# The end of the feature stage of a spectral-mixing and GLU kernel: another bank and another order for the left-over rows of the last group

## The chip, the cores and the metric

One core of one Trainium2 chip runs the kernel. The metric is the device time of one launch, in microseconds (us). Five engines work side by side, each in its own program order: TensorE (PE; its weight loads are listed apart as PEld), VectorE (DVE), ScalarE (ACT), GpSimd (POOL) and SyncE (SP), which issues most DMA transfers.

## The reference

A sequence `x` of 2048 tokens with 640 features goes through two residual blocks; all data are 32-bit floats.

```
h   = x + irfft2( rfft2(layernorm(x)) * (w_r + i w_i) )
z   = layernorm(h)
h2  = h + ((z Wg) * (z Wu)) Wd          # Wg, Wu: 640 x 1728, Wd: 1728 x 640
```

The two-dimensional Fourier transforms are done as products with constant tables. Only the first line matters here, and of it the filter (the product with `w_r + i w_i`), the inverse transform over the sequence and the beginning of the inverse transform over the features.

## The kernel before, in words

The spectral block has these stages. First, for 16 token tiles `t`, a product over the 128 tokens of a tile (line 261, `s1_mm`). Then the stage that the change touches: a loop over 16 groups `g` of frequencies (lines 569 to 646). For one group it does

- `d_mm(g)`: the transform over the features, into two PSUM banks with the tags `re` and `im`;
- `d_out(g)`: ScalarE copies them to SBUF;
- `s2_mm(g)`: the transform over the sequence within the group (line 465), two results of 128 x 322 for the two halves `h` of a group. For the last two groups, 14 and 15, they lie in banks `re` (half 0) and `im` (half 1);
- the filter: `y = v * w` (the direct product), the crossed product `us`, and their sum `y + us` (the join). For groups 0 to 13 this is `filt`. For the last two it is `filt_half` (line 493), by halves: half 1 of group 14 and half 0 of group 15 have the crossed product made by two ScalarE copies (lines 507, 508) and one GpSimd product (line 509), with the direct product on VectorE (line 498); half 0 of group 14 and half 1 of group 15 are done wholly on VectorE (lines 501 to 505);
- `is2_mm(g)`: the inverse transform within the group (line 512). For each half, one product for the 65 left-over rows, into `pr`, and two for the 128-row main parts, into `pm`. Group 14 takes `y` and `us` as two summands, so it needs no join and has 12 products; group 15 has 6. Each 32-bit product stands as two weight loads and two matmuls in the trace;
- `is2_parts(g)`: the results go from PSUM to SBUF. `main` (m) copies `pm` to `qm` on ScalarE; `high` (h) writes the rounded left-over rows to `qr`; `low` (l) writes the rest, `pr - high`, on VectorE; `end` (e) copies the 65th row on ScalarE; `edges` (g) splits that row in two. In the code the five of group 14 are `h0, e0, l0, m0, g0`, those of group 15 `h1, e1, l1, m1, g1`.

The next stage is the inverse transform over the features, for token tiles `t` (lines 721 to 763). `id_mm(0)` is its first work on TensorE: four products that read the columns of all groups in `qm` (8 loads and matmuls), then five that read `qr`, the last three of them with the 65th row. Its result has the tag `eo`, a pair of banks.

PSUM has eight banks. `banks(key, name)` (line 93) closes the pool that had the key and opens another in its place; key `a` is the left half, key `y` the right. In the feature stage pool `a` holds two banks of tag `re` and two of `im`, pool `y` one bank of `im2`, one of `ir2` and the pair `u`. Before the change `is2_mm(15)` writes `im2` and `ir2`, as did `is2_mm(13)`; `is2_mm(14)` writes the pair `u`. Pool `a` is closed and opened anew for `eo` at line 876, after all the lines of the change; pool `y` at line 877. The pools are opened with `tc.tile_pool(name=..., bufs=2, space=..., side=...)` and nothing more.

The order is written by hand: each engine runs its instructions in the order of the code. In the last turn of the loop (`g` = 14) it is: `s2_mm(14)`, `s2_mm(15)`, the filter of 14's half 0 with `is2_out(12)` inside it, `is2_mm(13)`, the three other halves of the filter, `is2_out(13)`; then `is2_mm(14)`, `is2_mm(15)` and the lines 636 to 645.

Of the kernel before, what the change touches and what calls it, by code (L numbers as in the profile page):

```python
# [19 lines left out]
NG = 16  # L20
# [58 lines left out]
def tile_spectral_glu(ctx: ExitStack, tc: tile.TileContext, x, wre, wim, wgu, wlast, wdown, wdlast,  # L79
                      cc, ci, fmain, frem, imain, irem, mm, out):  # L80
    nc = tc.nc
# [18 lines left out]
    def bank(tag, bufs=2):  # L100
        return pools["y" if tag in ("im2", "ir2") else "a"].tile([P, 512], F32, tag=tag, name=tag, bufs=bufs)
# [10 lines left out]
    def wk(shape, name):  # L112
        return work.tile(shape, F32, tag="wk", name=name)
# [20 lines left out]
    def home(tag, shape, name, dt=F32):  # L134
        return keep.tile(shape, dt, tag=tag, name=name)

    def cut(t, o, *shape):
        v = t[:, o:o + int(np.prod(shape))]
        names = [f"d{i}" for i in range(len(shape))]
        return v.rearrange(f"p ({' '.join(names)}) -> p {' '.join(names)}", **dict(zip(names[1:], shape[1:])))  # L140
# [156 lines left out]
    def rest_high(a, b):  # L297
        act(s1r[:, 0, a:b], rest[:, a:b], AF.Copy)

    def rest_low(a, b):  # L300
        tt(s1r[:, 1, a:b], rest[:, a:b], f32(s1r[:, 0, a:b]), op=OP.subtract)
# [15 lines left out]
    for ts, when, aside, root in GROUPS:  # L317
        k = len(when)
        fs, cs = front(ts, k)
        late = []  # L320
# [84 lines left out]
    def load_w(g):  # L405
        w, j = wts[:, g % 3], g // 2 if g < NG - 2 else g - 7
        i = wts[:, 5 if j == 8 else 3 + j % 2]
        nc.sync.dma_start(w, wre[g])
        if g % 2 == 0 or g >= NG - 2:
            nc.sync.dma_start(i, wim[j])  # L410
        W2[g] = w, i

    def load_mm(g, way):
        if g < NG:
            nc.sync.dma_start(mms[g % 4][:, way], mm[g][:, way])
# [10 lines left out]
    def d_mm(g):  # L426
        ps = PD[g] = bank("re"), bank("im")
        where = ((1, 0), (0, 0), (1, 160), (0, 160))
        main = [(b, o, FW[c], s1[:, c, g], fmt[:, FOFF[c]:FOFF[c] + FW[c]]) for c, (b, o) in enumerate(where)]
        if g not in ST:  # L430
            parts(ps, main, [(b, s1r[:, k, g], frt[:, l, b]) for k, l in ((0, 0), (0, 1), (1, 0)) for b in range(2)])
            return
        parts(ps, main, [])
        for q, ((b, o), w) in enumerate(zip(RWHERE, RW)):
            a = 4 * NQ + sum(RW[:q])
            mmx(ps[b][:, o:o + w], ST[g][0:99, q], frall[0:99, a:a + w], False, q >= 2)
# [28 lines left out]
    def s2_mm(g):  # L465
        if g >= NG - 2:
            ps = PU[g] = bank("re"), bank("im")
        elif g == 0:
            ps = PU[g] = bank("im2", 1), bank("ir2", 1)
        else:  # L470
            PU[g] = pools["y"].tile([P, 2, 512], F32, tag="u", name="u", bufs=1)
            ps = PU[g][:, 0], PU[g][:, 1]
        for h in range(2):
            nc.tensor.matmul(ps[h][:, 0:NQ], mms[g % 4][:, 0, h], T[g][:, h], start=True, stop=True)  # L474

    def filt(g):
        w, i = W2[g][0], W2[g][1][64 * (1 - g % 2):64 * (2 - g % 2)]
        y = Y[g] = wk([P, 2, NQ], "y")
        us = wk([P, 2, NQ], "us")

        def products(h, v):
            tt(y[:, h], v, w[:, h], op=OP.mult)
            nc.vector.scalar_tensor_tensor(us[0:64, h], v[64:128], -1.0, i[:, h], op0=OP.mult, op1=OP.mult)
            tt(us[64:128, h], v[0:64], i[:, h], op=OP.mult)

        if g:
            products(slice(0, 2), PU[g][:, :, 0:NQ])
        else:
            for h in range(2):
                products(h, PU[g][h][:, 0:NQ])  # L490
        return lambda: (tt if g else nc.gpsimd.tensor_tensor)(y, y, us, op=OP.add)

    def filt_half(g, h, alone=False, mid=()):
        if h == 0:
            Y[g] = wk([P, 2, NQ], "y"), wk([P, 2, NQ], "us")
        y, us = (a[:, h] for a in Y[g])
        v, w, im = PU[g][h][:, 0:NQ], *W2[g]
        direct = lambda: tt(y, v, w[:, h], op=OP.mult)
        join = lambda: tt(y, y, us, op=OP.add)
        if alone:  # L500
            direct()
            for f in mid:
                f()
            nc.vector.scalar_tensor_tensor(us[0:64], v[64:128], -1.0, im[64:128, h], op0=OP.mult, op1=OP.mult)
            tt(us[64:128], v[0:64], im[0:64, h], op=OP.mult)
            return direct, join
        act(us[0:64], v[64:128], AF.Copy, scale=-1.0)
        act(us[64:128], v[0:64], AF.Copy)
        nc.gpsimd.tensor_tensor(us, us, im[:, h], op=OP.mult)
        return direct, join  # L510

    def is2_mm(g):
        if g == NG - 2:
            both = pools["y"].tile([P, 2, 512], F32, tag="u", name="u", bufs=1)
            pm, pr = both[:, 0], both[:, 1]
        else:
            pm, pr = bank("im2", 1), bank("ir2", 1)
        PI[g] = pm, pr

        def o(ps, n, c, h):  # L520
            return ps[0:n, c * 256:(c + 1) * 256].rearrange("p (a m) -> p a m", m=8)[:, :, 4 * h:4 * h + 4]

        def mm(out, h, a, b):
            ys = [Y[g]] if g < NG - 2 else Y[g] if g == NG - 2 else Y[g][:1]
            for n, y in enumerate(ys):
                nc.tensor.matmul(out, y[:, h, a:b], inv(g, h), start=n == 0, stop=n == len(ys) - 1)  # L526

        if g < NG - 2:
            for h in range(2):
                mm(o(pr, 65, 0, h), h, 128, 193)  # L530
        for h in range(2):
            if g >= NG - 2:
                mm(o(pr, 65, 0, h), h, 128, 193)
            mm(o(pm, P, 0, h), h, 0, 128)
            mm(o(pm, P, 1, h), h, 193, 321)

    def inv(g, h):
        return mms[g % 4][:, 1, h].rearrange("p (a m) -> p a m", m=4)
# [22 lines left out]
    def is2_out(g):  # L561
        high, end, low, main, edges = is2_parts(g)
        high(copy)
        end(copy)
        low()
        main(slice(0, 4))
        edges(nc.gpsimd)
# [11 lines left out]
    for g in range(NG - 1):  # L579
        s2_mm(g)  # L580
        load_mm(g + 4, 0)
        if g + 2 < NG:
            d_mm(g + 2)
        if g + 3 == NG:
            xt = home("big", [P, 2, 5, 2, 512], "xt", F32R)
            flat = xt[:, 1].rearrange("p k l n -> p (k l n)")
            irt, sirt = cut(flat, 0, 5, NQ), cut(flat, 5 * NQ, 4, 162)
            scrap, near = cut(flat, 2258, D), cut(flat, 2258 + D, 4, 4, P)
        if g == NG - 2:
            nc.gpsimd.dma_start(flat[:, 0:2258], irem)  # L590
        if g == NG - 2:
            s2_mm(g + 1)
            filt_half(g, 0, True, (lambda: is2_out(g - 2),))
        if g >= 1:
            is2_mm(g - 1)
            load_mm(g + 3, 1)
        if g < NG - 2:
            add = filt(g)
        else:
            late = [filt_half(g, 1), filt_half(g + 1, 0), filt_half(g + 1, 1, True)]  # L600
            for f in (late[0][0], late[1][0], late[1][1], late[2][1]):
                f()
        if g + 3 < NG:
            load_w(g + 3)
        if g >= 4 and g in AGAIN:
            stack(*AGAIN[g])
        if g == 0:
            rest_high(MID, NG)
        elif g == 1:
            rest_low(MID, NG)  # L610
            qr = home("qr", [P, 2, NT, P], "qr", F32R)
        if g + 2 < NG:
            d_out(g + 2, (0,))
            if 1 <= g < NG - 3:
                high, end, low, main, edges = is2_parts(g - 1)
                high(copy)
                end(copy)
            d_out(g + 2, (1,))
            add()
            if 1 <= g < NG - 3:  # L620
                low()
                main(slice(0, 4))
                edges(nc.gpsimd)
        elif g == NG - 2:
            is2_out(g - 1)
        if g < 2:
            stack(*AGAIN[g])
        elif g == 2:
            spread(MID, NG)
        if g == 9:  # L630
            nc.sync.dma_start(cit, ci)
            nc.sync.dma_start(imt, imain)
# [3 lines left out]
    h0(copy)  # L636
    e0(copy)
    m0(slice(0, 4))
    h1(nc.vector.tensor_copy)
    l0()  # L640
    g0(nc.gpsimd)
    l1()
    m1(slice(0, 2), slice(2, 4))
    e1(copy)
    g1(nc.vector)
    make_identity(nc, ident)
# [289 lines left out]
    late = None  # L936
    for t in range(NT):
# [27 lines left out]
        if t == NT - 2:  # L965
            late = gate_parts(NC - 1, 0)
# [227 lines left out]
    for n, (blk, p) in enumerate(steps):  # L1194
        if p == 6:
            if blk == 0:
# [15 lines left out]
                late = gate_parts(NC - 2, 0)  # L1212
# [4 lines left out]
                late = gate_parts(NC - 1, 1)  # L1217
# [6 lines left out]
            else:  # L1224
# [60 lines left out]
                late = gate_parts(NC - 1, 0)  # L1285
# [15 lines left out]
                late = gate_parts(NC - 2, 0)  # L1301
# [250 lines left out]
```

## Time and profile before

| what | value |
|---|---|
| median of 3 runs | 673.8 us (673.65 to 674.02) |
| the profiled execution's own time | 673.84 us |
| its span, first to last instruction | 672.1 us |
| TensorE busy | 662.1 us (99%) |
| VectorE / ScalarE / GpSimd busy | 470.4 / 322.9 / 393.1 us |
| granted TensorE clock, mean | 1.000 |

Times in the trace count from the span's start. A row of the timeline gives the start and the length in us, the engine, the line, the operation with what it writes and reads, how many instructions are merged, and in brackets how long the engine stood idle just before and what ended that. Most matmuls stand under the line of a helper (L119).

### The profile page before, as it was taken

How to read it: one execution, taken by the hardware profiler on the slowest of the kernel's cores; microseconds unless marked ns; L12 is line 12 of the kernel's file. 1: busy time of each engine (PE TensorE's matmuls, PEld its weight loads, DVE VectorE, ACT ScalarE, POOL GpSimd, SP SyncE). 2: the span in 40 equal slices, each digit the busy share in tenths (PEclk: the TensorE clock that was granted, in tenths of full speed). 3: DMA queues.
4: the chain of work that ended last, by engine and by line, in shares of the span. 5: the costliest groups of instructions: out<-in, count | busy, mean ns of one | idle time of the engine just before them, and what ended most of it. 6: DMA issues, size and time to landing. Idle time of an engine off the chain costs nothing.

```text
span 672.1 us, 10248 instructions
## 1 busy us (share of the span) xinstructions
PE 662.1 (99%) x3695; PEld 587.1 (87%) x3695; DVE 470.4 (70%) x952; ACT 322.9 (48%) x622; POOL 393.1 (58%) x377
## 2 busy tenths in 40 slices
PE   6999999999999999999999999999999999999997
PEld 6999989888888888888888899788888888888887
DVE  6969996788757868594858566754747575756654
ACT  6977773585525253463626146634434252525220
POOL 3101224750397978878787445198787878787610
PEclk9999999999999999999999999999999999999999
DMA  9639885502212121042332467212002121212004
GB/s 320 224 113 283 246 249 149 157 1 79 78 40 79 39 79 35 16 115 53 102 74 79 99 134 257 79 40 78 11 29 79 40 78 40 79 40 80 1 1 156
DMA packets 48953, 66.12 MB, mean 98 GB/s; under 512 B 24082, under 2 KB 30670, under 8 KB 48774
## 3 DMA queue, kind: packets, MB, share of 16 engines
q1 hardware_dynamic: 48246, 62.91, 30.3%
q0 software_dynamic: 288, 2.16, 0.8%
q8 instruction: 29, 0.48, 0.3%
q10 hardware_dynamic: 368, 0.39, 0.2%
q14 instruction: 22, 0.18, 0.1%
HBM read 54.61 MB, written 10.84 MB: 97 GB/s over the span
## 4 chain that ended last, share of the span: by engine, by line
PE 95%; ACT 2%; DVE 2%; DMA 1%; issue 0%; DVEq 0%
PE e L119 50%; PE d L119 26%; PE eo L119 4%; PE y L119 2%; PE re L119 2%; PE u L474 2%; PE im L119 2%; PE im L526 2%; PE im L268 2%; PE ir L526 1%; DMA x<-in_x_dram 1%; ACT s L294 1%; ACT fold L210 0%; ACT fold L209 0%; PE y L792 0%; ACT bits L283 0%
## 5 line engine op out<-in xcount | busy, mean ns | idle before, releaser
L119 PE MATMUL e<-xt,wst 128*128 128x512 f32 x864 | 213.2, 391 | 0.0
L119 PEld LDWEIGHTS e<-xt,wst 128*128 128x128 f32 x864 | 159.8, 188 | 30.6
L1071 DVE TENSOR_TENSOR x<-d,x 128x320 f32<-128x320 f32 x280 | 123.4, 483 | 51.6 <-PE d L119 47.4
L119 PE MATMUL d<-wd,ht 128*128 128x320 f32 x832 | 143.6, 308 | 0.0
L119 PEld LDWEIGHTS d<-wd,ht 128*128 128x128 f32 x832 | 131.1, 188 | 7.6
L985 POOL TENSOR_TENSOR wst<-raw,wst 128x1024 fp32r<-128x1024 f32 x23 | 55.4, 2410 | 67.6 <-ACT wst L984 49.6
L119 PE MATMUL e<-t,wst 128*128 128x512 f32 x360 | 94.3, 392 | 0.0
L119 PEld LDWEIGHTS e<-t,wst 128*128 128x128 f32 x360 | 66.3, 188 | 12.6
L119 PE MATMUL d<-wt,ht 128*128 128x320 f32 x360 | 69.5, 310 | 0.0
L1001 POOL TENSOR_TENSOR wst<-raw,wst 128x896 fp32r<-128x896 f32 (+1 forms) x46 | 65.1, 1439 | 0.2 <-ACT wst L996 0.2
L119 PEld LDWEIGHTS d<-wt,ht 128*128 128x128 f32 x360 | 57.3, 188 | 2.4
L1087 ACT ACTIVATE ht<-e 128x512 fp32r<-128x512 f32 x44 | 26.4, 599 | 51.4 <-DVE e L1150 25.9
L1126 ACT ACTIVATE h<-e 128x512 f32<-128x512 f32 x24 | 14.3, 595 | 66.8 <-PE e L119 66.8
L1046 DVE TENSOR_TENSOR x<-d,x 128x320 f32<-128x320 f32 x62 | 27.5, 485 | 23.1 <-PE d L119 23.1
L996 ACT ACTIVATE wst<-raw 128x896 fp32r<-128x896 f32 (+1 forms) x48 | 30.2, 677 | 27.2 <-POOL raw L990 26.5
L677 ACT ACTIVATE wd<-draw 128x320 fp32r<-128x320 f32 (+1 forms) x30 | 15.7, 558 | 57.1 <-POOL draw L687 54.3
L119 PE MATMUL e<-xt,wdir 128*128 128x512 f32 x180 | 42.4, 393 | 0.0
L119 PEld LDWEIGHTS e<-xt,wdir 128*128 128x128 f32 x180 | 33.3, 188 | 8.1 <-ACT xt L802 0.5
L1146 DVE TENSOR_TENSOR e<-e,h 128x512 f32<-128x512 f32 x24 | 16.8, 699 | 30.8 <-PE e L119 17.8
L1090 DVE TENSOR_TENSOR ht<-e,ht 128x512 fp32r<-128x512 f32 x54 | 36.9, 685 | 1.6 <-ACT ht L1087 1.3
L656 POOL TENSOR_TENSOR wd<-draw,wd 128x640 fp32r<-128x640 f32 x8 | 12.4, 1579 | 40.9 <-ACT wd L655 40.9
L1143 ACT ACTIVATE h<-e 128x512 f32<-128x512 f32 x24 | 14.3, 597 | 40.1 <-PE e L119 40.1
(236 smaller groups left out, 1187.6 us busy)
## 6 DMA issues: line engine op xcount, KB each, us to landing
raw<-in_wgu_dram SPq DMA_DIRECT2D x24, 640.0 KB
draw<-in_wdown_dram SPq DMA_DIRECT2D x24, 320.0 KB
wts<-in_wre_dram SPq DMA_DIRECT2D x16, 322.0 KB
x<-in_x_dram SPq DMA_DIRECT2D x15, 320.5 KB
out_dram<-x SPq DMA_DIRECT2D x15, 320.0 KB
bits<-in_mm_dram SPq DMA_DIRECT2D x32, 128.0 KB
wts<-in_wim_dram SPq DMA_DIRECT2D x9, 322.0 KB
zfar<-zr SPq DMA_DIRECT2D x32, 80.0 KB
```

Source lines behind the costliest of these rows:

```text
L119: nc.tensor.matmul(o, l, r, start=start, stop=stop, skip_group_check=True)
L526: nc.tensor.matmul(out, y[:, h, a:b], inv(g, h), start=n == 0, stop=n == len(ys) - 1)
L677: act(o[:, 0, a:a + n], src, AF.Copy)
L985: ptt(wa[:, 1], stage[:, 0:1024], f32(wa[:, 0]), op=OP.subtract)
L996: act(ws[:, 0, o:o + b - a], stage[:, a:b], AF.Copy)
L1001: ptt(ws[:, 1, o:o + b - a], stage[:, a:b], f32(ws[:, 0, o:o + b - a]), op=OP.subtract)
L1046: tt(xv, ps[b][:, 0:320], xv, op=OP.add)
L1071: tt(xv, o, xv, op=OP.add)
L1087: act(hop[:, a, 0], src, AF.Copy)
L1090: engine.tensor_tensor(hop[:, a, 1], src, f32(hop[:, a, 0]), op=OP.subtract)
L1126: act(h0, oa, AF.Copy)
L1146: tt(ob, ob, h1, op=OP.add)
```

## The change

`is2_mm(15)` takes a bank of tag `im` for `pr` instead of `ir2`, and in its second half the products for the left-over rows come last. In the filter, the direct product of group 14's half 1 is put on VectorE ahead of the work for group 15. At the end, `h1` goes behind `l0` and `m1`.

```diff
@@ is2_mm
         else:
-            pm, pr = bank("im2", 1), bank("ir2", 1)
+            pm, pr = bank("im2", 1), bank("ir2", 1) if g < NG - 1 else bank("im")
@@
         for h in range(2):
-            if g >= NG - 2:
+            last = g == NG - 1 and h
+            if g >= NG - 2 and not last:
                 mm(o(pr, 65, 0, h), h, 128, 193)
             mm(o(pm, P, 0, h), h, 0, 128)
             mm(o(pm, P, 1, h), h, 193, 321)
+            if last:
+                mm(o(pr, 65, 0, h), h, 128, 193)
@@ the loop over g
         else:
-            late = [filt_half(g, 1), filt_half(g + 1, 0), filt_half(g + 1, 1, True)]
-            for f in (late[0][0], late[1][0], late[1][1], late[2][1]):
+            direct, _ = filt_half(g, 1)
+            direct()
+            late = [filt_half(g + 1, 0), filt_half(g + 1, 1, True)]
+            for f in (*late[0], late[1][1]):
                 f()
@@ after the loop
     m0(slice(0, 4))
-    h1(nc.vector.tensor_copy)
     l0()
     g0(nc.gpsimd)
+    m1(slice(0, 2), slice(2, 4))
+    h1(nc.vector.tensor_copy)
     l1()
-    m1(slice(0, 2), slice(2, 4))
     e1(copy)
     g1(nc.vector)
```

## Rows read from the trace of the kernel before

**Rows 1.** The page's part 1: busy time of each engine.

```profile
PE 662.1 (99%) x3695; PEld 587.1 (87%) x3695; DVE 470.4 (70%) x952; ACT 322.9 (48%) x622; POOL 393.1 (58%) x377
```

**Rows 2.** Busy time in stretches: length, PE, PEld, DVE, ACT, POOL, clock, DMA share, GB/s.

```profile
107.10:152.00 44.90, 44.90 (x281) 39.82 (x282) 35.58 (x83) 25.90 (x55) 26.12 (x32) 1.00 0.35 98
```

**Rows 3.** Timeline of TensorE's weight loads at the end of the feature stage.

```profile
102.48 0.30 PEld L526 LDWEIGHTS u<-bits,y 128*128 128x128 f32 x2
102.70 0.30 PEld L526 LDWEIGHTS u<-bits,us 128*128 128x128 f32 x2
103.20 0.19 PEld L526 LDWEIGHTS u<-bits,y 128*65 128x65 f32 x2 [0.19 <-DVE y L498]
...
105.05 0.19 PEld L526 LDWEIGHTS ir<-bits,y 128*65 128x65 f32 x2 [0.50 <-DVE qr L559]
...
107.07 0.98 PEld L119 LDWEIGHTS eo<-tab,qm 128*128 128x128 f32 x7 [0.66 <-ACT qm L552]
```

**Rows 4.** The chain that ended last, same stretch: start, length, what.

```profile
106.15 0.46 PE im L526 x4
...
106.63 0.39 ACT qm L552
...
107.07 7.62 PE eo L119 x52
```

**Rows 5.** Timeline of VectorE, same stretch.

```profile
101.12 0.49 DVE L498 TENSOR_TENSOR y<-im,wts 128x322 f32<-128x322 f32 x1
...
102.65 0.49 DVE L498 TENSOR_TENSOR y<-im,wts 128x322 f32<-128x322 f32 x1
103.06 0.48 DVE L498 TENSOR_TENSOR y<-re,wts 128x322 f32<-128x322 f32 x1
103.65 0.90 DVE L499 TENSOR_TENSOR y<-y,us 128x322 f32<-128x322 f32 x2
104.58 0.42 DVE L559 TENSOR_TENSOR qr<-ir,qr 64x256 fp32r<-64x256 f32 x1
106.19 0.42 DVE L558 CAST qr<-ir 64x256 fp32r<-64x256 f32 x1 [1.19 <-PE ir L526]
...
106.98 0.41 DVE L559 TENSOR_TENSOR qr<-ir,qr 64x256 fp32r<-64x256 f32 x1
107.80 0.21 DVE L555 CAST qr<-bits 1x128 fp32r<-1x128 f32 x1 [0.42 <-ACT bits L541]
108.05 0.28 DVE L556 TENSOR_TENSOR qr<-bits,qr 1x128 fp32r<-1x128 f32 x1
```

**Rows 6.** Timeline of ScalarE, same stretch.

```profile
100.70 0.43 ACT L508 ACTIVATE us<-im 64x322 f32<-64x322 f32 x1
...
104.78 0.38 ACT L541 ACTIVATE qr<-u 64x256 fp32r<-64x256 f32 x1 [1.43 <-PE u L526]
...
105.46 0.60 ACT L552 ACTIVATE qm<-u 128x512 f32<-128x512 f32 x1
...
107.50 0.27 ACT L541 ACTIVATE bits<-ir 1x128 f32<-1x128 f32 x1 [0.21 <-POOL qr L555]
```

**Rows 7.** Timeline of GpSimd: the crossed products of 14's half 1 and 15's half 0.

```profile
101.26 1.72 POOL L509 TENSOR_TENSOR us<-us,wts 128x322 f32<-128x322 f32 x2 [0.32 <-POOL qr L556]
```

**Rows 8.** Timelines at the next closing of pool `a`, where `gu` opens the third stage.

```profile
150.33 0.70 ACT L802 ACTIVATE xt<-y 128x640 fp32r<-128x640 f32 x1 [0.85 <-PE y L792]
...
150.40 0.81 DVE L763 TENSOR_TENSOR x<-eo,x 128x640 f32<-128x640 f32 x1
...
151.33 3.29 PEld L119 LDWEIGHTS e<-xt,wdir 128*128 128x128 f32 x15 [0.46 <-ACT xt L802]
```

**Rows 9.** Who waited for whom on SP's queue, 95 to 135 us: total, times, longest.

```profile
SPq L705 <- DVE qr L558: 9.2, 1, 9.2
```

**Rows 10.** An idle stretch early in the span: stretch by stretch (columns as rows 2), TensorE's timeline.

```profile
10.00:12.00 2.00, 0.46 (x4) 0.49 (x5) 1.90 (x11) 1.97 (x7) 0.74 (x2) 1.00 1.04 395
...
11.54 1.60 PE L268 MATMUL im<-bits,fold 128*128 128x128 f32 x12 [1.55 <-DVE bits L285]
```

## The prediction, made before the changed kernel ran

> **What bounds the kernel now.** I read the busy times first: TensorE works 99% of the span [rows 1]. Then the stretches: from 107.10 to 152.00 it is busy for 44.90 of 44.90 us [rows 2]. So once `id_mm(0)` has begun, at 107.07, nothing but TensorE sets the pace, and what moves that start moves the end by as much. The question is therefore only when `id_mm(0)` starts. The weight loads just before it show three waits [rows 3]: the second half of `is2_mm(14)` (103.20) for a direct product of VectorE, `is2_mm(15)` (105.05) for the `low` of group 13, and `id_mm(0)` (107.07) for ScalarE's `m1`. The reader is to see that each wait is short (0.19, 0.50 and 0.66 us in these rows). The change aims at the first two; the third then has another cause.
>
> **The change part by part.** It removes and adds no instruction and no transfer; it moves some. I follow each engine.
>
> *The direct product of 14's half 1.* It stood at 102.65 and goes to the place at 101.12 [rows 5]. It reads a bank that ScalarE copies from until 100.70 + 0.43 = 101.13 [rows 6], so it starts at about 101.16, against VectorE's turn at 101.12: 0.04 us lost. Queued behind it are the three VectorE steps of 15's half 1, then 15's direct product and the joins. From the first of the five filter steps to the first join it was 103.65 - 101.12 = 2.53 us [rows 5]; the same five instructions stand there in another order, so the join comes at 103.69. Pairs of steps follow each other by 0.41 (102.65 to 103.06) up to 0.59 (103.06 to 103.65), so I allow 0.1 more: 103.69 to 103.80. It ends 0.49 later, at 104.18 to 104.29.
>
> *The second half of `is2_mm(14)`.* Its direct product is now there at 101.65, its crossed product at 102.12, half of GpSimd's 1.72 us from 101.26 [rows 7]. Two loads start every 0.22 us (102.48, 102.70), so the next was due at 102.92 and came at 103.20 [rows 3]: 0.28 us are won. `is2_mm(14)` ends that much earlier: ScalarE, which followed it at 104.78 [rows 6], can go at 104.50, and TensorE's next load is due 12 x 0.11 after 102.92, about 104.2.
>
> *`is2_mm(15)` in another bank.* It no longer waits for the `low` of group 13 (104.58 + 0.42 = 105.00 [rows 5]); the reader of the `im` bank that it takes is the product moved ahead, done by 101.65. What is late next is the first join: 104.18 to 104.29, and 0.06 to the load (102.65 + 0.49 = 103.14 to 103.20 above). So it starts at 104.24 to 104.35 and not at 105.05, 0.70 to 0.81 us earlier. The second join, 0.41 behind the first, is there before the sixth load. The end, 106.61 [rows 4], becomes 105.80 to 105.91, now with `pr` last; `pm` is ready two loads, 0.22 us, earlier. The order inside costs nothing by itself.
>
> *`m1`.* ScalarE needs from 104.78 to 105.46 + 0.60 = 106.06 for group 14 [rows 6]; 0.28 us earlier, it is free at 105.78, when `pm` is ready (105.58 to 105.69). So `m1` starts at 105.79 instead of 106.63. From there to `id_mm(0)` it was 0.44 us [rows 4]: by the data of `qm`, `id_mm(0)` could start at 106.23, 0.84 us earlier.
>
> *The pool.* Here I choose. `pr` of group 15 lay in pool `y`, which is not needed again before `is1_mm(0)`. Now it lies in pool `a`, and pool `a` is closed and opened anew directly ahead of `id_mm(0)`. The pools are opened without the argument `reuse_waits`, whose default is "pool" (the other value is "tile"): what takes the place of a closed pool waits for the readers of all its tiles. The trace has one such switch where the readers come late [rows 8]: the first load of `gu` came at 151.33, its data from ScalarE were there at 151.03, and VectorE's last read of the closed pool's `eo` ended at 150.40 + 0.81 = 151.21, 0.12 us ahead. The row names ScalarE, which had been done for 0.30 us; the reader of the closed pool is the closer one. So the last reader of `pr` gates `id_mm(0)`. That reader is `e1`, behind `l1`, behind `h1`:
>
> - `h1` follows the end of `pr` by 0.03, as `m1` followed 106.61 [rows 4]: 105.83 to 105.94, and takes 0.42 [rows 5];
> - `l1` needs its output. Between a VectorE step and the next that reads it there are 0.04 us (107.80 + 0.21 to 108.05) to 0.11 (103.06 + 0.48 to 103.65) [rows 5]: 106.29 to 106.47, and takes 0.41. Before, `l0` filled this gap, and `l1` came 0.79 behind `h1`; now 0.46 to 0.53;
> - `e1` came 0.11 behind the end of `l1` (106.98 + 0.41 = 107.39 to 107.50 [rows 5, 6]), though the row names GpSimd: 106.81 to 106.99, and takes 0.27;
> - TensorE follows by 0.05 (105.00 to 105.05 [rows 3, 5]) to 0.12 [rows 8]: **107.13 to 107.38**, against 107.07.
>
> So of 0.84 us nothing is left, and 0.06 to 0.31 us are lost. I take 0.15, near the low end, since the same pair `l1`, `e1` stands in the rows and the small gaps are those of single waits.
>
> *What else is moved.* `l0` goes ahead of `h1`, to about 105.1, and with it GpSimd's `g0`, which waits for it: earlier by over 1 us, and nobody waits. `g1` (0.21 + 0.28 on VectorE [rows 5]) ends near 107.6; its readers on TensorE come after the eight loads on `qm`, over 0.9 us behind 107.13, so it stays covered. If `id_mm(0)` began at 106.23 that cover would shrink to nothing and cost some 0.1 us. SP's queue is moved past nothing: its spread of `qr` waited 9.2 us for `h1` [rows 9] and starts 0.3 us earlier, with TensorE never idle in that stretch [rows 2]. Nothing is gained there.
>
> *The sum.* The profiled execution took 673.84 us, 0.04 above the median of 673.8. +0.15 on it is 673.99, or **673.95** as a median.
>
> **The rivals.** *Bank by bank.* The wait at the switch is only for the banks that `eo` takes: `id_mm(0)` begins at 106.23, and 0.84 less 0.1 for `g1` leaves -0.75, 673.05. For it speaks that in rows 8 the late reader may have sat in the very bank that the first load needed, so those rows can't tell bank from pool. Against it speaks the default named above. The Trainium skill's page "PSUM — Partial Sum Buffer", section on bank collisions, asks to guard PSUM by bank and quadrant, which is this rival's rule; no row here shows which one the program keeps.
>
> *Slower: the clock.* TensorE would stand still from 105.85 to 107.2, some 1.35 us in one piece, where before it had waits of 0.50 and 0.66 us with work between them [rows 3]. If the granted clock fell from 2.4 to 1.2 GHz, the products behind it, 7.62 us from 107.07 to 114.69 [rows 4], could take up to twice as long, so up to 681.4; a fifth of that would be enough to be seen. It decides from an idle stretch longer than the trace already has: early in the span TensorE idled 1.55 us, and the clock of that stretch is 1.00 [rows 10], the upper level. The Trainium skill's page "TensorE: Matmul & The Clock Gate", Part 1, says that throttled is the default state and that activity releases it, which speaks against any change that gathers idle time. By rows 10 the gap is too short.
>
> *The change does not do what it says.* The join may come so late that `is2_mm(15)` gains nothing; then the chain to `e1` would end about 0.7 us later, at 107.9 to 108.1, and the time would be about 674.7. The five steps of VectorE [rows 5] speak against it.
>
> **How the numbers follow.** The pool's wait, with +0.06 to +0.31, has 0.83; bank by bank 0.11; the late join 0.03; the clock 0.02; 0.01 is left for a gain beyond all this. A measurement of this kernel can tell about 0.2% from no change, 1.35 us. The pool's wait, the bank rival (-0.75) and the late join (+0.9) lie within that. So within 0.2% has 0.97, slower 0.02, faster 0.01. The likeliest case has 673.7 to 674.3, with the spread of the runs before (673.65 to 674.02) around 673.95. The range takes in the bank rival and ends short of the late join: 672.9 to 674.5.
>
> **What would show it.** Right: the first direct product near 101.16, the joins from about 103.7, `is2_mm(15)` at 104.2 to 104.4 with no wait for a `low`, `m1` at 105.8, and then the first load on `eo` at 107.1 to 107.4, some 0.1 us behind `e1`. Wrong: that load at 106.2 to 106.4 while `l1` or `e1` still runs (bank by bank), matmuls longer than before with a clock under 1.00, or `is2_mm(15)` at 105 again.

## The result and the profile after

The changed kernel took 674.7 us (median of 22 runs, 674.27 to 675.22), the kernel before, beside it on the same chip, 673.65 (22 runs). The ratio is 1.0014, with a 95% interval of 1.0008 to 1.002. By the 0.2% of the prediction that is no difference; but the interval lies wholly above 1, so a small loss is there. The time lies 0.2 us above the predicted range. The profiled execution took 675.22 us, with a span of 673.4.

The busy times first, then two stretches. Page, part 1, and the windows of the kernel after (columns as in [rows 2]):

```profile
PE 662.0 (98%) x3695; PEld 587.2 (87%) x3695; DVE 470.3 (70%) x952; ACT 322.7 (48%) x622; POOL 393.0 (58%) x377
...
107.90:152.80 44.90, 44.90 (x281) 39.81 (x282) 35.27 (x82) 25.32 (x53) 24.99 (x29) 1.00 0.34 98
105.90:107.90 2.00, 0.23 (x3) 0.00 (x0) 1.27 (x4) 1.04 (x4) 1.34 (x5) 1.00 0.02 7
```

Every engine works as long as before, within 0.2 us [rows 1], and behind `id_mm(0)` TensorE is busy for 44.90 of 44.90 us as it was [rows 2]. New is the second window: TensorE has work for 0.23 of 2.00 us. The clock in it, and behind it, is 1.00.

**A measure that does not depend on the launch.** The starts of two profiled executions differ by some tenths of a microsecond for reasons that lie ahead of the change. So everything here counts from the first product of `s2_mm(14)`, which stands ahead of all that is changed. TensorE's timeline, the kernel before, then its weight loads at `id_mm(1)`:

```profile
98.20 0.71 PE L474 MATMUL re<-t,bits 128*128 128x322 f32 x2
...
108.87 1.16 PEld L119 LDWEIGHTS eo<-tab,qm 128*128 128x128 f32 x8
```

The same for the kernel after, with the loads of `is2_mm(14)`, `is2_mm(15)`, `id_mm(0)` and `id_mm(1)`, then the first products of `id_mm(0)`:

```profile
98.47 0.71 PE L474 MATMUL re<-t,bits 128*128 128x322 f32 x2
...
103.20 0.25 PEld L526 LDWEIGHTS u<-bits,y 128*65 128x65 f32 x2
...
104.53 1.36 PEld L526 LDWEIGHTS im<-bits,y 128*65 128x65 f32 x12
107.90 1.12 PEld L119 LDWEIGHTS eo<-tab,qm 128*128 128x128 f32 x8 [2.02 <-ACT bits L544]
108.97 0.77 PEld L119 LDWEIGHTS eo<-xt,qr 128*128 128x128 f32 x5
109.70 0.47 PEld L119 LDWEIGHTS eo<-tab,qm 128*128 128x128 f32 x3
...
107.90 1.37 PE L119 MATMUL eo<-tab,qm 128*128 128x161 f32 x8 [1.77 <-ACT bits L544]
```

I call two distances the *stretch*: to the first load of `id_mm(0)`, before 107.07 - 98.20 = 8.87 [rows 3], after 107.90 - 98.47 = 9.43; and to the first load of `id_mm(1)`, 10.67 and 11.23. Both grew by 0.56 us. The two waits of [rows 3] at 103.20 and 105.05 are gone; at `id_mm(0)` stands one of 2.02 where it was 0.66 (1.77 for the products, which end later than their loads), and what ended it is ScalarE's `end` of group 15 (L544, the `e1` of the prediction).

Who made `e1` late is in the chain of waits of the kernel after (start, length, what):

```profile
105.52 0.60 ACT qm L555
...
106.15 0.42 DVE qr L562
...
106.60 0.43 DVE qr L561
...
107.05 0.43 DVE qr L562
...
107.58 0.28 ACT bits L544
...
107.90 0.68 PE eo L119 x3
```

It reads: ScalarE's `m0`, then VectorE's `l0`, `h1`, `l1`, then `e1`, then `id_mm(0)`. VectorE's timeline shows the same link from its side:

```profile
101.44 0.89 DVE L498 TENSOR_TENSOR y<-im,wts 128x322 f32<-128x322 f32 x2
...
103.97 0.90 DVE L499 TENSOR_TENSOR y<-y,us 128x322 f32<-128x322 f32 x2
104.90 0.42 DVE L562 TENSOR_TENSOR qr<-ir,qr 64x256 fp32r<-64x256 f32 x1
106.15 0.42 DVE L562 TENSOR_TENSOR qr<-u,qr 64x256 fp32r<-64x256 f32 x1 [0.83 <-ACT qm L555]
106.60 0.42 DVE L561 CAST qr<-im 64x256 fp32r<-64x256 f32 x1
107.05 0.42 DVE L562 TENSOR_TENSOR qr<-im,qr 64x256 fp32r<-64x256 f32 x1
```

VectorE is free at 105.32, and `l0` (reads `u`) waits 0.83 us for ScalarE's `m0`. `m0` reads `u` too: its `pm` and the `pr` that `l0` needs are the two banks of one tile of group 14. In the kernel before the same `l0` came behind `h1`, with no wait of its own:

```profile
106.64 0.42 DVE L559 TENSOR_TENSOR qr<-u,qr 64x256 fp32r<-64x256 f32 x1
```

ScalarE's timeline of the kernel after gives `m0`, `m1` and `e1`:

```profile
105.52 0.60 ACT L555 ACTIVATE qm<-u 128x512 f32<-128x512 f32 x1
106.01 0.66 ACT L555 ACTIVATE qm<-im 128x256 f32<-128x256 f32 x2
107.58 0.27 ACT L544 ACTIVATE bits<-im 1x128 f32<-1x128 f32 x1 [0.92 <-DVE qr L562]
```

**A second loss, 180 us later.** 0.56 us is not all: the medians are 1.05 us apart here, and 0.82 in a repeat. Following one and the same instruction through both traces, the distance stays at 0.80 to 0.83 from 108 us on, and jumps to 1.14 near 286 us. VectorE's timeline in the third stage (the products with `Wg`, `Wu` and `Wd`), with the product of TensorE that comes behind it, the kernel before, then after:

```profile
284.53 0.69 DVE L1156 TENSOR_TENSOR h<-e,h 128x512 f32<-128x512 f32 x1 [0.61 <-PE e L119]
285.33 0.70 DVE L1158 TENSOR_TENSOR e<-e,h 128x512 f32<-128x512 f32 x1
...
291.57 0.68 PE L119 MATMUL d<-wt,ht 128*128 128x320 f32 x3
```

```profile
285.33 0.69 DVE L1161 TENSOR_TENSOR h<-e,h 128x512 f32<-128x512 f32 x1 [0.62 <-PE e L119]
286.47 0.70 DVE L1163 TENSOR_TENSOR e<-e,h 128x512 f32<-128x512 f32 x1 [0.46 <-DVE h L1161]
...
292.72 0.68 PE L119 MATMUL d<-wt,ht 128*128 128x320 f32 x3 [0.21 <-DVE x L1076]
```

The second of the two followed the first by 0.80 us and now follows by 1.14, though it waits for nothing but VectorE itself. VectorE is then behind with `x`, and TensorE waits for `x` at 292.72, where before it did not. The change edits nothing in this stage. It does alter the number of VectorE's instructions ahead of this place: the compiled program has 1153 of them instead of 1151. The two more are instructions that only wait on a semaphore, which neither count nor show in the rows. In the trace of the kernel after, one of them stands just ahead of the moved direct product, the other just ahead of `l0`.

### The profile page after: what moved, and what is told of

It is laid out like the page before. It is cut to its first block, busy times and chain, and to the rows that moved or that the text cites. A ratio compares the mean times of both kernels' runs of the same rounds, so it can differ in the third digit from the quotient of the medians.

```text
span 673.4 us, 10250 instructions
## 1 busy us (share of the span) xinstructions
PE 662.0 (98%) x3695; PEld 587.2 (87%) x3695; DVE 470.3 (70%) x952; ACT 322.7 (48%) x622; POOL 393.0 (58%) x377
## 4 chain that ended last, share of the span: by engine, by line
PE 89%; ACT 3%; DVE 3%; DMA 3%; POOL 1%; issue 1%; SPq 0%; DVEq 0%; ACTq 0%
PE e L119 47%; PE d L119 24%; PE eo L119 4%; PE y L119 2%; PE re L119 2%; PE u L474 2%; PE im L119 2%; PE im L526 2%; PE im L268 2%; DMA z<-zfar 1%; PE ir L526 1%; DMA raw<-in_wgu_dram 1%; DMA x<-in_x_dram 1%; ACT s L294 1%; ACT fold L210 0%
```

## The experiments

Twelve kernels ran, each with 11 timed runs beside 33 of the kernel before. This table sums them up; the sections after it give edit, expectation and reading. "Stretch" is to `id_mm(0)` and to `id_mm(1)`; "sum" is the second stretch less 10.67, plus 0.33 where VectorE's gap near 286 us is there (the distance above grows by that, from about 0.81 to 1.14); "time" is the median less that of the kernel before (673.70 in the first four, 673.74 in the next four, 673.73 in the last).

| run | stretch | VectorE instr. | gap | sum | time | ratio, 95% |
|---|---|---|---|---|---|---|
| a1 after again | 9.43, 11.23 | 1153 | yes | +0.89 | +0.82 | 1.0002 to 1.002 |
| a2 `h1` first | 9.00, 10.80 | 1152 | no | +0.13 | +0.12 | 0.9993 to 1.0011 |
| a3 waits by tile | 7.97, 10.51 | 1153 | yes | +0.17 | +0.17 | 0.9992 to 1.001 |
| a4 both | 7.97, 10.43 | 1152 | no | -0.24 | -0.16 | 0.9989 to 1.0006 |
| b1 bank alone | 9.10, 10.90 | 1151 | no | +0.23 | +0.28 | 0.9993 to 1.0011 |
| b2 bank back | 8.69, 10.81 | 1153 | yes | +0.47 | +0.50 | 0.9999 to 1.0016 |
| b3 before, plus 2 | 8.86, 10.66 | 1153 | yes | +0.32 | +0.42 | 0.9997 to 1.0014 |
| b4 after, plus 1 | 9.42, 11.23 | 1154 | no | +0.56 | +0.51 | 1.0 to 1.0017 |
| c1 direct alone | 8.91, 10.70 | 1152 | no | +0.03 | -0.07 | 0.999 to 1.0008 |
| c2 `pr` last | 7.97, 10.37 | 1152 | no | -0.30 | -0.39 | 0.9984 to 1.0002 |
| c3 `pr` last, `l1` first | 7.97, 10.44 | 1152 | no | -0.23 | -0.31 | 0.9985 to 1.0003 |
| c4 `l0` ahead of `m0` | 9.01, 10.80 | 1153 | yes | +0.46 | +0.40 | 0.9996 to 1.0014 |

Most single intervals take in 1, so one time alone says little. That the sum out of the traces and the median agree within 0.10 us in all twelve is what carries the reading.

### The change again, and `h1` ahead of `l0`

The changed kernel once more 

> The changed kernel once more, as a yardstick for the three beside it. In its first profile the stretch from the first product of s2_mm(14) to the first load of id_mm(0) was 9.43 us (98.47 to 107.90) against 8.87 before (98.20 to 107.07), and to the first load of id_mm(1) 11.23 against 10.67: +0.56 us in the stretch. The median was 1.05 us above before. Theory 1 (all of the loss is in the stretch): 0.5 to 0.6 us over before, and the 0.5 us more that the first profile shows behind 107.9 (at about 290 us and at the turn of the blocks at about 400 us) were chance. Theory 2 (part of it comes later, each time): again about 1 us, with steps of 0.2 to 0.4 us behind id_mm(0).

And with `l0` behind the work on group 15:

```diff
     m0(slice(0, 4))
-    l0()
-    g0(nc.gpsimd)
     m1(slice(0, 2), slice(2, 4))
     h1(nc.vector.tensor_copy)
     l1()
+    l0()
+    g0(nc.gpsimd)
     e1(copy)
```

> The changed kernel with h1 and l1 ahead of l0 on VectorE. Theory (l0 waits for ScalarE's m0, and h1 and l1 stand behind it, so e1, for which the new pool waits, comes late): h1 starts right behind the end of is2_mm(15), about 7.70 us into the stretch instead of 8.13, l1 at 8.16, e1 at 8.7, the first load of id_mm(0) at 9.0 instead of 9.43; the time is 0.4 to 0.45 us below the changed kernel, still 0.1 to 0.6 above before. Rival (id_mm(0) is held by something other than the chain h1, l1, e1): the first load stays at 9.4 and the time with the changed kernel's.

The repeat has the same stretches, 9.43 and 11.23, and the same gap, so the second theory holds: part of the loss comes later, each time. With `h1` first the stretch is 9.00, 0.43 shorter. The weight loads of that run:

```profile
107.50 1.12 PEld L119 LDWEIGHTS eo<-tab,qm 128*128 128x128 f32 x8 [1.58 <-ACT bits L544]
```

`e1` still ends the wait. So 0.43 of the 0.56 us is `l0`'s place, and 0.13 remains for the way over `h1`, `l1`, `e1` that the prediction had priced at 0.15. That the time fell by more than 0.43 (from +0.82 to +0.12) is the gap near 286 us: it is gone in this run, which has one VectorE instruction less, the wait ahead of `l0`.

### The pool's wait taken away

All PSUM pools are opened with the argument that lets the wait at a closing go tile by tile:

```diff
-            tc.tile_pool(name=name, bufs=2, space=bass.MemoryType.PSUM, side="right" if key == "y" else "left"))
+            tc.tile_pool(name=name, bufs=2, space=bass.MemoryType.PSUM, side="right" if key == "y" else "left",
+                         reuse_waits="tile"))
```

> The changed kernel with the PSUM pools opened with reuse_waits="tile", so that a new pool's tile waits for the readers of what lay in its own banks only. Theory (the pool as a whole is waited for): id_mm(0) starts behind m1, 8.0 us into the stretch instead of 9.43, but its last three products then wait for g1, so that id_mm(1) starts at 10.6 instead of 11.23: 0.6 us below the changed kernel, about level with before. Rival (the wait was for the bank, not the pool): nothing changes, 9.43 and 11.23 stay.

Weight loads of this run:

```profile
106.33 1.12 PEld L120 LDWEIGHTS eo<-tab,qm 128*128 128x128 f32 x8 [0.56 <-ACT qm L556]
107.41 0.32 PEld L120 LDWEIGHTS eo<-xt,qr 128*128 128x128 f32 x2
108.46 0.45 PEld L120 LDWEIGHTS eo<-xt,qr 128*128 128x128 f32 x3 [0.74 <-POOL ident masks.py:199]
108.87 1.16 PEld L120 LDWEIGHTS eo<-tab,qm 128*128 128x128 f32 x8
```

`id_mm(0)` now follows `m1`, and the stretch falls from 9.43 to 7.97: the wait of 2.02 us was the closing of pool `a`. But the third load of `qr`, one that needs the 65th row, stands still for 0.74 us. The row names GpSimd; the step that makes what the load reads is VectorE's `g1`, which ends about 0.1 us ahead of it in this trace. So of 0.90 us gained at `id_mm(0)` (7.97 against 8.87 before) only 0.16 is left at `id_mm(1)`, and VectorE's gap (0.33) takes more than that.

Both edits together:

> Both: h1 and l1 ahead of l0, and waits tile by tile. Theory: id_mm(0) starts at 8.0, g1 ends about 9.6 us into the stretch, so the last three products of id_mm(0) wait little, and id_mm(1) starts at 10.1 to 10.2 against 10.67 before and 11.23 after: 1.0 to 1.1 us below the changed kernel and about 0.5 below before. Rival (the two edits remove the same wait and don't add up): level with the better of the two alone.

The stretch is again 7.97; `id_mm(1)` is at 10.43, later than expected, and the time is 0.16 us under before instead of 0.5. `g1` began 0.44 us earlier than with the waits by tile alone, but ended only 0.08 earlier: its two steps took 0.34 and 0.56 us (see the last section).

### The bank alone, and all but the bank

The kernel before with only the bank changed:

```diff
-            pm, pr = bank("im2", 1), bank("ir2", 1)
+            pm, pr = bank("im2", 1), bank("ir2", 1) if g < NG - 1 else bank("im")
```

> The kernel before, with one edit: `pr` of group 15 lies in the bank `im` (pool `a`) instead of `ir2` (pool `y`). Measured from the first product of `s2_mm(14)` to the first load of `id_mm(0)`: 8.87 us in the kernel before, 9.43 in the one after. Theory (the switch of pool `a` waits for the last reader of `pr` of group 15, `e1`, behind `l1`): `is2_mm(15)` no longer waits for the `low` of group 13 and starts about 104.5 instead of 105.05, but `h1`, `l0`, `l1` and `e1` must now be over before `id_mm(0)`: h1 105.9, l0 106.4, l1 106.8, e1 107.3 to 107.6, `id_mm(0)` about 107.65. The stretch becomes 9.4 to 9.6, the time 0.5 to 0.7 us more than before. VectorE has as many instructions as before (1151), so its extra gap near 286 us should be absent. Rival (the new order of work on VectorE and TensorE costs the time, not the bank): the stretch is 8.87 or shorter and the time that of before or less.

The kernel after with only that line undone:

> The kernel after, with `pr` of group 15 back in the bank `ir2` (pool `y`). Theory: nothing of pool `a` is read late any more, so the first load of `id_mm(0)` waits for `m1` (ScalarE) and not for `e1`; in exchange `is2_mm(15)` waits again for the `low` of group 13 (about 105.3 on the clock of the kernel after, 0.85 us later than there). Stretch to `id_mm(0)` 8.7 to 8.95 (after 9.43, before 8.87); `id_mm(1)`, which needs the small edges of group 15 behind `l0`, `h1`, `l1`, may come 0 to 0.3 later than before. If the extra gap of VectorE near 286 us (0.33 us) goes by the number of VectorE's instructions, it is there, since this kernel has 1153 as the one after has: then +0.3 to +0.6 us against before in all. Rival (the gap goes by the order of the feature stage's end, not by the number): no gap, -0.1 to +0.3.

Weight loads with the bank alone, at `id_mm(0)`:

```profile
107.41 1.12 PEld L119 LDWEIGHTS eo<-tab,qm 128*128 128x128 f32 x8 [1.42 <-ACT bits L541]
```

and with the bank back, at `is2_mm(15)` and `id_mm(0)`:

```profile
105.22 0.19 PEld L526 LDWEIGHTS ir<-bits,y 128*65 128x65 f32 x2 [0.76 <-DVE qr L562]
...
107.02 1.12 PEld L119 LDWEIGHTS eo<-tab,qm 128*128 128x128 f32 x8 [0.49 <-ACT qm L555]
```

The bank decides who ends the wait: `e1` (bits) with it, `m1` (qm) without. Alone it makes the stretch 0.23 us longer, so the expected 0.5 to 0.7 was too much. Of the steps written there `h1` came 0.24 earlier and `e1` 0.32 earlier (105.77 and 107.09, less the 0.11 by which this trace starts later than that of before). With the bank back the stretch is 8.69, a little under that of before, and `is2_mm(15)` waits for the `low` of group 13 again; but `id_mm(1)` is 0.14 later than before, behind `l0`, `h1`, `l1` and `g1`. So the new order of the copies loses with either bank: in `im`, one edit apart, `id_mm(1)` is at 11.23 against 10.80 with `h1` first; in `ir2` it is at 10.81 against 10.70 (below, the direct product alone), where the order of the products differs too.

### `l0` ahead of `m0`

The most direct trial of what `l0` waits for:

```diff
-    m0(slice(0, 4))
     l0()
+    m0(slice(0, 4))
     g0(nc.gpsimd)
```

> The kernel after, with `l0` ahead of `m0` in the written order (bank, products and pool as in the kernel after). Theory (the readers of one PSUM tile on two engines are run one after the other in the written order): `l0` waits for `e0` only and starts about 0.6 us earlier than in the kernel after, `m0` now waits for `l0`: it starts 0.4 to 0.5 us later than there. `h1` follows the end of `is2_mm(15)` at once, 0.4 earlier than in the kernel after, and `l1` too; but ScalarE does `m0` and `m1` first and comes to `e1` late. Stretch 9.0 to 9.35 (after 9.43). VectorE has 1153 instructions, so the extra gap of 0.33 us near 286 us is there: time 0.5 to 0.8 us above before. Rival (`l0` waits for something else): `m0` is where it was in the kernel after and `l0` too, stretch 9.43.

VectorE's `l0`, ScalarE's `m0` and the loads of `id_mm(0)` in this run:

```profile
105.20 0.42 DVE L562 TENSOR_TENSOR qr<-u,qr 64x256 fp32r<-64x256 f32 x1 [0.23 <-ACT bits L544]
```

```profile
105.65 0.60 ACT L555 ACTIVATE qm<-u 128x512 f32<-128x512 f32 x1 [0.48 <-DVE qr L562]
```

```profile
107.14 1.12 PEld L119 LDWEIGHTS eo<-tab,qm 128*128 128x128 f32 x8 [1.60 <-ACT bits L544]
```

Now `l0` goes as soon as `e0` is over, and `m0` waits for `l0`. The two only read, they read different banks, and neither needs the other's output. So these two readers of one PSUM tile, on two engines, are made to run one after the other, in the written order. Readers of two tiles are not: in the kernel before, where `pm` and `pr` of group 15 are tiles of their own, `m1` is written behind `l1` and started at 106.63 [rows 4], 0.35 us ahead of `l1` at 106.98 [rows 5]. The Trainium skill's page "PSUM — Partial Sum Buffer", section on bank collisions, asks for a guard by bank and quadrant. The trace shows one that is wider, over both banks of the tile. The stretch is 9.01, 0.42 less than in the kernel after, the same as with `h1` first; the time, 0.40 above before, is a little under the 0.5 to 0.8 expected.

### The gap near 286 us

Two small writes of a constant into a column that nothing reads are added to the kernel before, one to the kernel after, on VectorE where it idles:

```diff
     make_identity(nc, ident)
+    for _ in range(2):
+        nc.vector.memset(eps[:, 15:16], EPS)
```

> The kernel before, with two small writes of a constant into an unused column added on VectorE behind the identity, where VectorE idles: 1153 VectorE instructions, as in the kernel after, instead of 1151. The end of the feature stage is that of before: stretch 8.87, `id_mm(1)` at 10.67. Theory (the extra gap of VectorE near 286 us, between the product of column 5 on `h` and that on `e`, goes by the place of these instructions in VectorE's stream): the gap of 0.3 to 0.5 us is there, TensorE waits for `x` behind it, and the time is 0.33 us more than before. Rival (the gap belongs to what the change does in the feature stage): no gap, and the time of before within 0.1.

> The kernel after, with one small write of a constant into an unused column added on VectorE behind the identity, where VectorE idles: 1154 VectorE instructions. The stretch is that of the kernel after (9.43; `id_mm(1)` at 11.23). Theory (the gap near 286 us goes by the place in VectorE's stream): with one more instruction ahead, it falls one instruction earlier, to a place where VectorE waits anyway, or stays between the same two; in the first case the time is 0.55 us above before, in the second 0.9. Rival (the gap belongs to what the change does): 0.9, as after.

VectorE near 286 us, the kernel before with two more instructions, then the kernel after with one more:

```profile
284.74 0.69 DVE L1158 TENSOR_TENSOR h<-e,h 128x512 f32<-128x512 f32 x1 [0.62 <-PE e L119]
285.89 0.70 DVE L1160 TENSOR_TENSOR e<-e,h 128x512 f32<-128x512 f32 x1 [0.46 <-DVE h L1158]
```

```profile
284.97 0.69 DVE L1163 TENSOR_TENSOR h<-e,h 128x512 f32<-128x512 f32 x1 [0.61 <-PE e L119]
285.76 0.70 DVE L1165 TENSOR_TENSOR e<-e,h 128x512 f32<-128x512 f32 x1
```

The kernel before gets the gap (1.15 us from start to start) and costs 0.42 us more; the kernel after loses it (0.79) and costs 0.51 instead of 0.82. Over all fourteen traces the gap is there in the six with 1153 instructions and in none of the eight with 1151, 1152 or 1154. So it goes by where these instructions stand in VectorE's stream, and not by what the feature stage does; but it was the wait ahead of `l0` that moved them there. What in the stream makes the gap is not shown: the two small queues that the page lists as kind "instruction" carried nothing from 285 to 288 us in the kernel before or after.

### The direct product alone, and a version with the gain kept

The kernel before with only the direct product of 14's half 1 moved:

> The kernel before, with one edit: the direct product of 14's half 1 goes ahead on VectorE; bank, order of the products and order of the copies are those of before. Theory: the second half of `is2_mm(14)` starts 0.28 us earlier, but `is2_mm(15)` still waits for the `low` of group 13, which stands behind the joins and moves by no more than 0.1, so it starts about as before; nothing of pool `a` is read late. Stretch from the first product of `s2_mm(14)` to `id_mm(0)` 8.85 to 9.0 (before 8.87), `id_mm(1)` at 10.65 to 10.8, time within 0.15 of before. VectorE has 1152 instructions, so no extra gap near 286 us. Rival (the earlier end of `is2_mm(14)` moves `m0`, `m1` and the start of `id_mm(0)` with it): stretch 8.6, time 0.28 less.

The stretch is 8.91: the product ahead gives nothing while `is2_mm(15)` waits for the `low` of group 13.

A version that keeps the gain without the bank has `pr` of group 15 in `ir2`, the copies in the order of before, the direct product ahead as in the change, and in `is2_mm(15)` all products into `pr` behind those into `pm`, so that the `low` of group 13 has time. Of its edits the last, set against the kernel after:

```diff
         for h in range(2):
-            last = g == NG - 1 and h
-            if g >= NG - 2 and not last:
+            if g == NG - 2:
                 mm(o(pr, 65, 0, h), h, 128, 193)
             mm(o(pm, P, 0, h), h, 0, 128)
             mm(o(pm, P, 1, h), h, 193, 321)
-            if last:
+        if g == NG - 1:
+            for h in range(2):
                 mm(o(pr, 65, 0, h), h, 128, 193)
```

> A version meant to keep the gain and drop the loss: the direct product ahead as in the change, `pr` of group 15 in the bank `ir2` of pool `y` as before, the copies in the order of before (m0, h1, l0, g0, l1, m1, e1, g1), and in `is2_mm(15)` the products into `pr` of both halves last, behind all those into `pm`. Theory: `is2_mm(15)` starts with `pm` as soon as the first join is there (6.06 us behind the first product of `s2_mm(14)`, as in the kernel after), and comes to `pr` 0.9 us later, when the `low` of group 13 is over; `m1` follows `m0` without a gap and `id_mm(0)` follows `m1`, since no reader of pool `a` is late. Stretch 7.95 to 8.15 (after 9.43, before 8.87); `g1` ends about when the loads of `qr` come, so `id_mm(1)` at 9.75 to 10.05 (before 10.67); VectorE has 1152 instructions, no extra gap. Time 0.6 to 0.9 us less than before. Rival (a gain at the start of `id_mm(0)` is taken back whole by the wait for `g1`): `id_mm(1)` at 10.4 or later, time 0.2 less at most.

Its loads of `id_mm(0)` and `id_mm(1)`, then VectorE's last step of `g1`:

```profile
106.22 1.12 PEld L119 LDWEIGHTS eo<-tab,qm 128*128 128x128 f32 x8 [0.55 <-ACT qm L555]
107.29 0.33 PEld L119 LDWEIGHTS eo<-xt,qr 128*128 128x128 f32 x2
108.21 0.44 PEld L119 LDWEIGHTS eo<-xt,qr 128*128 128x128 f32 x3 [0.59 <-POOL ident masks.py:197]
108.62 1.16 PEld L119 LDWEIGHTS eo<-tab,qm 128*128 128x128 f32 x8
```

```profile
107.81 0.28 DVE L559 TENSOR_TENSOR qr<-bits,qr 1x128 fp32r<-1x128 f32 x1
```

`id_mm(0)` starts 0.90 us earlier than before, near the 0.84 that the prediction had for `qm` alone. `g1` ends at 108.09 and the third load of `qr` follows at 108.21, so 0.60 of it is taken back: 10.37 instead of the expected 9.75 to 10.05. In working that out I had let `h1` start behind the loads of `pr`; it starts behind the end of its products, 0.3 later. The rival of that expectation, that the wait for `g1` takes the whole gain, was nearer in the start of `id_mm(1)` (10.4 or later). The time is 673.34 us, the lowest of all, 0.39 under the kernel before and not 0.6 to 0.9; the interval of the ratio still holds 1, so the gain rests on the trace.

With `l1` ahead of `l0` in that version:

> As the run with `pr` last, but with `l1` ahead of `l0` and `g0`. Theory: `e1` comes directly behind `m1`, 0.3 us earlier, and `g1` with it, but GpSimd's `g0`, which waits for `l0`, now runs beside VectorE's `g1`, whose two small steps take up to 0.9 us together instead of 0.5 when both engines run such steps at a time. `id_mm(1)` at 9.75 to 10.15; time within 0.2 of the run with `pr` last, on either side. Rival (the two engines don't hinder each other): 0.1 to 0.2 us less than the run with `pr` last.

`e1` comes 0.33 us earlier, but `g1`, whose two steps take 0.33 and 0.56 us here, ends 0.07 later, and `id_mm(1)` is at 10.44, behind the 9.75 to 10.15 expected: the rival is out.

## Why the prediction was wrong

The starts below are those of the kernel after less 0.27 us (98.47 - 98.20), to stand beside the forecast.

- **The direct product** was forecast at 101.16 and came at 101.17; the joins at 103.69 to 103.80, came at 103.70. Right.
- **`is2_mm(14)`** lost its wait, its half 1 starting at 102.93 (forecast 102.92). **`is2_mm(15)`** was forecast at 104.24 to 104.35 without a wait and came at 104.26. Right.
- **`m1`** at 105.79: came at 105.74. Right. By the data of `qm`, `id_mm(0)` could go 0.84 us earlier: with the pool's wait taken away it went 0.90 earlier.
- **The pool's wait** takes all of that back, through `l1` and `e1`: right, by the releaser of the load and by the run with waits by tile. `l1` came 0.45 behind `h1` (forecast 0.46 to 0.53), `e1` 0.11 behind the end of `l1` (0.11), TensorE 0.05 behind `e1` (0.05 to 0.12): each link held.
- **The step that failed** is "`l0` goes ahead of `h1`, to about 105.1 … nobody waits". `l0` started at 105.88, because it waits for `m0`, and `h1`, `l1` and `e1` are queued behind it: `h1` came at 106.33 instead of 105.83 to 105.94. I counted who waits for `l0` and GpSimd's `g0`, and neither what `l0` itself waits for in its new place nor that the critical `h1` now stands behind it on VectorE. In the kernel before `l0` started at 106.64, when `m0` had been over since 106.06 [rows 6], so no row showed a wait. Even ahead of `m0` it would not have come at 105.1: with `e0` alone to wait for it came at 105.27 (105.20 in that run, whose trace starts 0.07 earlier). The wait for `m0` costs 0.43 us (9.43 against 9.00); the rest of the term is 0.13 where 0.15 was forecast.
- **Not in the sum at all** was VectorE's gap near 286 us, 0.33 us. The prediction argued that no instruction is added; the compiled program has two more on VectorE, that only wait, and one of them is `l0`'s.

The two together, 0.43 + 0.33 = 0.76, less 0.02 for the term that was over, make 673.95 into 674.69; 674.7 was measured. That it fits so closely is luck in part: the prediction counts from 673.8, and the kernel before took 673.65 beside the changed one. From there the traced losses are 0.13 + 0.43 + 0.33 = 0.89 us, against 1.05 measured and 0.82 in the repeat. By the sum of the prediction, either of the two alone would have left the time within the range.

**The rivals.** *Bank by bank* is out. Its price was wrong too: had there been no wait by pool, 0.16 us would have been left and not 0.75, since the third load on `qr` then stands still for 0.74 us behind `g1`, where the prediction charged 0.1. *The clock* did not fall: it is 1.00, the upper level, in the stretch in which the products stand still for 1.77 us, and behind it; [rows 10] had 1.55 us. The Trainium skill's page "TensorE: Matmul & The Clock Gate", Part 1, makes activity the condition for the upper clock. The trace shows no loss from this idle stretch. *The late join* did not happen, though its number, 674.7, is the one measured: a number met by another way shows nothing.

## What to carry to other kernels

When an instruction is moved forward on its engine, ask what it waits for in the new place as well as who waits for it: a wait that was long over in the old place leaves no row, and everything behind it on that engine pays. Look for other engines that read the same tile, even another bank of it, since such readers were run one after the other here. And a start that becomes early is worth only as much as the next thing that the same consumer needs; here 0.9 us at `id_mm(0)` was 0.16 to 0.30 at `id_mm(1)`.

## What the runs showed of the hardware that was not expected

**A gap that goes by the place in the stream.** The same two instructions of VectorE follow each other by about 0.80 us with 1151, 1152 or 1154 VectorE instructions in the program, and by about 1.14 with 1153. At 0.33 us on TensorE the gap is nearly as large as the 0.43 that the place of `l0` costs. Comparisons of a few tenths of a microsecond need a look at every stage, also those that were not edited.

**VectorE's steps on tiny operands take longer beside GpSimd's.** With `h1` first, GpSimd's `g0` and VectorE's `g1`, each two steps on a row of 128 elements, run at the same time. VectorE, then GpSimd, in that run:

```profile
107.48 0.34 DVE L558 CAST qr<-bits 1x128 fp32r<-1x128 f32 x1
107.85 0.56 DVE L559 TENSOR_TENSOR qr<-bits,qr 1x128 fp32r<-1x128 f32 x1
```

```profile
107.46 0.28 POOL L558 CAST qr<-bits 1x128 fp32r<-1x128 f32 x1 [1.24 <-DVE qr L562]
107.82 0.45 POOL L559 TENSOR_TENSOR qr<-bits,qr 1x128 fp32r<-1x128 f32 x1
```

VectorE's two steps take 0.34 and 0.56 us, where alone they took 0.21 and 0.28 [rows 5]; GpSimd's keep their 0.28 and 0.45. The same holds in the other two runs in which the two pairs coincide (both edits together, and `pr` last with `l1` first). The Trainium skill's page "GPSIMD Engine Reference", section 1, says that GpSimd shares its SBUF interfaces with VectorE and contends with its instructions that have two SBUF inputs. The second step is one, and it is the one that doubled; the first, with one input, went from 0.21 to 0.34 us, and no run here shows why.
